# The second FFN product of the last two batches and of the global rows with seven half-size products for eight, in a kernel whose orders are laid by a planner

## The chip, the cores and the metric

The kernel runs on one core of a Trainium2 chip. The metric is the device time of one execution in microseconds (us), the median of several runs. A profiled execution gives the trace; its own time differs a little from the median and is given beside it.

The engines are TensorE (PE: matmuls, PEld: weight loads), VectorE (DVE), ScalarE (ACT), GpSimd (POOL) and SyncE (SP, here the queue that issues stores and transposing DMAs).

## The reference

Eight batches, eight heads, 512 local and 32 global tokens of 64 elements for each. Global rows see every token, local rows see the 32 global tokens and the local ones at most 32 away. The attention's rows, 544 for each batch and 4352 in all, of 512 elements, go through a two-layer product with a gate:

```python
out_g = matmul(softmax(scale * q_g @ k_all^T), v_all)            # 32 global rows
mask  = abs(pos[:, None] - pos[None, :]) <= 32
s_l   = concat([scale * q_l @ k_g^T, where(mask, scale * q_l @ k_l^T, -1e9)])
out_l = matmul(softmax(s_l), concat([v_g, v_l]))                  # 512 local rows
x = concat([out_g, out_l], axis=2).transpose(0, 2, 1, 3).reshape(4352, 512)

h = x @ w_in                       # 512 -> 2048
g = h * clip(h + 3, 0, 6) / 6
out = g @ w_out                    # 2048 -> 512
```

## The kernel before, in words

**Order.** The program declares operations with `add(engines, costs, emit, deps, rank, ...)`: on which engine each may run, what it costs by a model, what it waits for and which buffers (`take`, `give`) it holds. `Plan.run` then plays the whole kernel forward in Python and so fixes the order of every engine; `pick` chooses TensorE's next piece by keys (`key()`, with the constants `KEYS`, `SLACK`, `STEP`, `LEAD`, `PACE`, `WAIT`, `LATE`), and for a step that two engines may do it takes the one that is free. The operations are then emitted in that order. On the chip each engine works through its own list, waiting on semaphores, and never reorders it.

**Attention of a batch b.** `loads(b)` brings q, k, v; q and k are turned to have the head's dimension on partitions: by TensorE in small blocks (`turn_qk`, L700), in wide blocks (`turn_wide`, L737, batches in `WIDE`), or by transposing DMAs (`turn_all`, batches in `QT`, here batch 7). `spread` copies the values `vn` into `vs`, where each block of 128 rows finds its windows (L643 to L645; which engine may copy is in `MOVERS`: GpSimd, for batches 6 and 7 GpSimd and ScalarE). `local(b, j)` makes, for each of the four blocks of 128 rows, the scores S (L819), the masked maximum (VectorE, L831), the exponentials (ScalarE, L835), the turn of E (by TensorE where `EM` or `ETURN` says so, L848, else by DMA, L363), the product A with the values (L862), the norm (VectorE, L874 and L876), and the turn of the result x into `xt` (X; `XM`, `XTURN`, L883). `global_(b)` does the same for the 32 global rows against all tokens (L921 to L965).

**FFN of a batch.** `ffn_local(b)` calls `first()` 16 times: four matmuls (L1003) of 512 columns into a PSUM bank `m`, a relu on ScalarE (L1009) and the gate on VectorE (L1013), which frees the bank and leaves 128 of the 2048 inner columns in `gl`. `second()` then makes, for each 128 rows, 16 matmuls of 512 columns (L1029), a copy out of PSUM (ScalarE L1040 or VectorE L1042) into one of three `ot` buffers, and a store (SyncE, L1075). `ffn_global()` does the same at the end for the 256 global rows of all batches together; a block of 128 of them belongs to four batches and is stored by four DMAs (L1090). The two FFN products of one batch lie between the attention of the next one, piece by piece.

**PSUM.** Eight banks: three `m`, two `s` (scores and turns), two `a` (A and turns), one `t` (turns), which is handed to `m` when the last turn is done. At the start, until the first product can run, `warm()` puts matmuls without use (L1149) into TensorE's list.

## Time and profile before

| | us |
|---|---|
| median of the runs (329.3, 330.81, 330.38) | 330.38 |
| the profiled execution's own time | 331.21 |
| its span in the trace | 329.4 |
| TensorE busy | 318.2 (97%) |
| VectorE busy | 239.3 (73%) |
| ScalarE busy | 237.2 (72%) |
| GpSimd busy | 174.9 (53%) |
| granted TensorE clock | 1.0 |
| first product's matmuls (L1003, all forms) | 133.4 |
| second product's matmuls (L1029, all forms) | 132.5 |

Matmuls run in a pipeline, so that the busy time of one (0.38 us for 512 columns) is longer than the distance from its start to the next one's. What a matmul costs TensorE is read from a row of many in sequence in the chain (start of the first to start of what follows, divided by their number). A name such as `m<-wout,gl` gives output and inputs; "x44" is a number of instructions.

### The profile page before, as it was taken

To read this page: it belongs to the slowest core of one execution; us is meant where nothing else is said; L and a number is where in the kernel's file an instruction comes from. 1 tells how busy PE (TensorE), PEld (TensorE's weight loads), DVE (VectorE), ACT (ScalarE), POOL (GpSimd) and SP (SyncE) were. 2 spreads that over 40 slices of the span, in tenths; PEclk is the share of its full clock that TensorE was granted. 3 is DMA by queue.
4 is the path that set the end of the run, shared out by engine and by line. 5 is a ranking of instruction groups with operands and counts; after the bars stand their busy time and mean duration, and the time that the engine had idled before them with its cause. 6 is when DMAs were issued, how large, how long until landed. Compare 5 with 4: busy or idle time off the path is not lost.

```text
span 329.4 us, 12254 instructions
## 1 busy us (share of the span) xinstructions
PE 318.2 (97%) x4880; PEld 164.4 (50%) x4880; DVE 239.3 (73%) x987; ACT 237.2 (72%) x571; POOL 174.9 (53%) x278
## 2 busy tenths in 40 slices
PE   8999968999899999999999999999999999999995
PEld 3456756654445544455444544444444444446644
DVE  5699998879985889878898997588414993376400
ACT  3799999848967688689768999979815982365511
POOL 8499353799548879979997998059200000000000
PEclk9999999999999999999999999999999999999999
DMA  8999999998999799959999999598934457200013
GB/s 128 226 204 173 178 235 217 123 180 182 113 136 158 143 116 168 170 120 180 179 111 128 211 102 140 123 136 105 177 99 121 60 109 120 82 34 0 34 57 103
DMA packets 111369, 44.30 MB, mean 134 GB/s; under 512 B 88304, under 2 KB 107088, under 8 KB 111312
## 3 DMA queue, kind: packets, MB, share of 16 engines
q0 software_dynamic: 53136, 17.47, 52.6%
q1 hardware_dynamic: 58176, 26.05, 43.2%
q8 instruction: 38, 0.62, 0.8%
q14 instruction: 19, 0.16, 0.2%
HBM read 35.13 MB, written 8.91 MB: 134 GB/s over the span
## 4 chain that ended last, share of the span: by engine, by line
PE 75%; ACT 9%; DMA 7%; DVE 5%; issue 2%; POOL 1%; ACTq 0%
PE m L1029 30%; PE m L1003 23%; PE t L1029 4%; ACT ex L835 4%; PE t L1003 3%; PE m L1149 3%; DMA win<-in_moe_w_in_dram 3%; PE a L862 3%; DMA et<-ex 3%; PE s L819 2%; ACT t L1009 2%; DVE gl L1013 2%; DMA vn<-in_v_l_dram 1%; ACT vs L643 1%; PE t L883 1%
## 5 line engine op out<-in xcount | busy, mean ns | idle before, releaser
L1003 PE MATMUL m<-xt,win 128*128 128x512 f16 (+1 forms) x536 | 114.3, 354 | 4.2 <-DVE gl L1013 3.1
L1029 PE MATMUL m<-wout,gl 128*128 128x512 f16 (+1 forms) x496 | 117.7, 376 | 0.1
L645 POOL COPY vs<-vn 64x528 f16<-64x528 f16 (+1 forms) x165 | 102.5, 621 | 22.0 <-ACT vn L381 5.7
L1013 DVE SCALAR_TENSOR_TENSOR gl<-t,m 128x512 f16<-128x512 f32 (+1 forms) x147 | 86.3, 601 | 24.2 <-ACT t L1009 23.8
L835 ACT ACTIVATE ex<-sm,mx 128x128 f16<-128x128 f32 x256 | 85.1, 396 | 14.6 <-DVE mx L831 14.1
L1009 ACT ACTIVATE t<-m 128x512 f32<-128x512 f32 (+1 forms) x147 | 76.7, 532 | 19.7 <-PE m L1003 18.7
L1003 PEld LDWEIGHTS <-win 128*128 128x128 f16 x640 | 59.7, 98 | 57.9 <-issue 4.7
L1029 PEld LDWEIGHTS <-gl 128*128 128x128 f16 x560 | 51.7, 98 | 53.5 <-issue 0.4
L831 DVE CUSTOM_DVE_ANT_0 sm<-s,mask 128x128 f32<-128x128 f32 x256 | 60.0, 285 | 7.2 <-PE s L819 5.9
L643 ACT COPY vs<-vn 32x528 f16<-32x528 f16 (+1 forms) x39 | 24.5, 628 | 0.8
L876 DVE TENSOR_TENSOR x<-a,rec 128x256 f16<-128x256 f32 x64 | 24.0, 416 | 0.0
L1040 ACT COPY ot<-m 128x512 f32<-128x512 f32 (+1 forms) x21 | 12.1, 576 | 15.7 <-PE m L1029 15.7
L353 POOL DMA_DIRECT2D vn<-in_v_l_dram x24 | 21.1, 888 | 1.3 <-DMA kn<-in_k_l_dram 0.8
L831 DVE DVE_READ_ACCUMULATOR2_ANT mx<- 128x1 f32 x256 | 21.2, 83 | 0.0
L353 POOL DMA_DIRECT2D vn<-in_v_g_dram x7 | 4.1, 581 | 25.4 <-PE a L965 24.5
L862 PE MATMUL a<-vs,et 128*32 128x65 f16 x1024 | 14.4, 195 | 1.3 <-DMA et<-ex 1.2
L1149 PE MATMUL m<-ident 128*128 128x512 f16 x57 | 15.6, 392 | 0.0
L862 PEld LDWEIGHTS <-et 128*32 128x32 f16 x1024 | 10.2, 96 | 10.9 <-issue 7.3
L1013 DVE SCALAR_TENSOR_TENSOR gl<-t,t 128x512 f16<-128x512 f32 (+1 forms) x13 | 8.1, 624 | 9.7 <-ACT t L1009 9.7
L1029 PE MATMUL t<-wout,gl 128*128 128x512 f16 (+1 forms) x64 | 14.8, 353 | 0.0
L874 DVE RECIPROCAL rec<-a 128x4 f32<-128x4 f32 x64 | 8.5, 167 | 7.9 <-PE a L862 7.9
L353 POOL DMA_DIRECT2D kn<-in_k_l_dram x22 | 14.1, 644 | 0.1
(108 smaller groups left out, 292.4 us busy)
## 6 DMA issues: line engine op xcount, KB each, us to landing
out_dram<-ot SPq DMA_DIRECT2D x31, 256.0 KB, 2.6
vs<-vn SPq DMA_DIRECT2D x14, 264.0 KB, 7.0
qn<-in_q_l_dram POOLq DMA_DIRECT2D x14, 256.0 KB, 8.1
kn<-in_k_l_dram POOLq DMA_DIRECT2D x14, 256.0 KB, 7.1
vn<-in_v_l_dram POOLq DMA_DIRECT2D x24, 128.0 KB, 5.8
win<-in_moe_w_in_dram POOLq DMA_DIRECT2D x4, 512.0 KB, 9.6
wout<-in_moe_w_out_dram POOLq DMA_DIRECT2D x8, 256.0 KB, 11.2
gl<-in_v_l_dram POOLq DMA_DIRECT2D x8, 128.0 KB, 9.3
```

The lines of the kernel that those rows point to most:

```text
L353: op = add("POOL", dma(rows, run), lambda: nc.gpsimd.dma_start(out=dst, in_=src), deps, rank, LOAD_LAT + (MARGIN if what[0] in "vqkg" and ...
L643: nc.scalar.copy(out=dst, in_=src)
L645: (nc.vector if o.on == "DVE" else nc.gpsimd).tensor_copy(out=dst, in_=src)
L831: nc.vector.tensor_tensor_reduce(out=sm[i3][h], in0=pss[e][:, p * P:(p + 1) * P], in1=m, scale=-scale, scalar=3.0e38, op0=ALU.add, op1=ALU ...
L835: nc.scalar.activation(out=ex[ie][:, h, :], in_=sm[i3][h], func=EXP, scale=-1.0, bias=mx[i3][h])
L862: nc.tensor.matmul(out=psa[h // 4][q, c0:c0 + D + 1], lhsT=et[k][:, h * P + u * Sg:h * P + (u + 1) * Sg], rhs=vs[r][:, j * UJ + u, h, 0:D ...
L876: nc.vector.tensor_tensor(out=xs[ix][:, 4 * c * D:4 * (c + 1) * D].rearrange("q (h d) -> q h d", d=D), in0=acc[c][:, :, 0:D], in1=rr[c].to ...
L1003: nc.tensor.matmul(out=ps[:, 0:n], lhsT=w_in[:, m, c * P:(c + 1) * P], rhs=x(m), start=(m == 0), stop=(m == NP - 1))
L1009: nc.scalar.activation(out=t1[st["t"]][:, 0:n], in_=pm[st["m"]][:, 0:n], func=RELU, bias=0.5, scale=1.0 / 6.0)
L1013: nc.vector.scalar_tensor_tensor(out=g, in0=t1[st["t"]][:, 0:n], scalar=1.0, in1=pm[st["m"]][:, 0:n], op0=ALU.min, op1=ALU.mult)
L1029: nc.tensor.matmul(out=pm[st["m"]][:, 0:n], lhsT=g[c][:, t0:t0 + P], rhs=w_out[:, c, cols], start=(c == 0), stop=(c == NDFF - 1))
L1149: nc.tensor.matmul(out=pm[slots["m"][0]], lhsT=w, rhs=x)
```

## The change

Three parts.

*Seven products for eight.* For the batches 6 and 7 and for the global rows, `ffn_local` and `ffn_global` no longer call `second()`. The gated matrix G (rows by 2048) and `w_out` (2048 by 512) are cut into halves each way, and the four quarters of the output are made from seven half-size products (Strassen's scheme in Winograd's form). One pair is 256 rows: two blocks of 128, one from the upper half of the rows, one from the lower. There are five pairs: two in batch 6, two in batch 7, one in the global rows. A pair is 7 products of 8 matmuls of 256 columns, where there were 2 x 16 matmuls of 512.

- Four sums of quarters of `w_out` (`weight_sums`, 128 partitions by 2048 elements, f16) go into the buffers of q and k (`qn`, `kn`), on GpSimd.
- Sums of the gated halves (`sevenths`, L1070 in the new file; four for each two chunks, f16, 128x512 for a batch and 128x256 for the global rows) go into the buffers of the windows' values (`vs`), on VectorE or GpSimd; the planner gave 21 to VectorE and 27 to GpSimd.
- `pair` adds the products' results: one copy and three additions (`plus`, L1134) into f32 buffers laid over `xt` and `qT`, and four additions (`outs`, L1147) that read a PSUM bank and write a quarter of 128x256 into an `ot` buffer. For a batch a quarter is one store (L1214), for the global rows four stores of 32x256 (L1240).

*Banks.* When the attention is done, the two `s` and the two `a` banks are handed to `m` as the `t` bank is.

*Orders laid anew.* The FFN of batch 6 is declared after the local attention of batch 7. The order of the loads (`ORDER`), the priorities of the first two batches (`OFF`), which turns of E and X go through TensorE (`EM`, `XM`, `ETURN`, `XTURN`), `QT` (empty: batch 7 is turned by TensorE), `WIDE` (without batch 2), `MOVERS` (batches 2 to 6 GpSimd alone, 7 GpSimd and VectorE; ScalarE in none of them) and the constants of `pick` are new, so that the whole kernel's order changes.

Counted in the orders of the two kernels: matmuls of the second product, 528 of 512 columns and 32 of 256 before, 384 and 280 after; window copies on ScalarE 39 and 7, on VectorE 13 and 24, on GpSimd 165 and 186; stores of 128x512 31 and 24, of 128x256 2 and 16, of 32x512 8 and 0, of 32x256 0 and 16.

```diff
@@ -385,20 +387,20 @@
-    ORDER = "q0 k0 id v0 w0 o4 Q bd v1 o6 o1 w1 K V G w3 o7 o3 o0 w2 o5 o2".split()
+    ORDER = "q0 k0 v0 bd w0 id o7 Q v1 w1 V K G o2 w2 o1 o6 o3 w3 o0 o4 o5".split()
-    EM, XM = {(b, j) for b in range(2) for j in range(4)}, set()
+    EM, XM = set(), {(0, 0), (0, 1)}
-    ETURN = "00000000 11101110 10111111 11111111"
-    XTURN = "00000000 11001001 00010110 11011111"
-
-    QT = (7,)
-    MOVERS = {b: ("POOL",) if b < 6 else ("POOL", "ACT") for b in range(2, 8)}
-
-    WIDE = (0, 1, 2)
+    ETURN = "00000000 11100110 11011011 01111111"
+    XTURN = "00000000 10111010 01111111 11111111"
+
+    QT = ()
+    MOVERS = {b: ("POOL",) if b < 7 else ("POOL", "DVE") for b in range(2, 8)}
+
+    WIDE = (0, 1)
...
+    SEVEN, SUMS = {6: 2, 7: 4, 8: 4}, ("DVE", "POOL")
...
+    def both(dst, a, b, op, n, engines, deps, rank, what):
+        o = add(engines, tuple(dve(n, 2) if e == "DVE" else 100.0 + 1.9 * n for e in engines), None, deps, rank, lat=220.0, what=what)
+
+        def emit():
+            (nc.vector if o.on == "DVE" else nc.gpsimd).tensor_tensor(out=dst, in0=a, in1=b, op=op)
+        o.emit = emit
+        return o
+
+    def weight_sums():
...
+        for k, (a, d, x) in enumerate(((w_out[:, lo, right], w_out[:, lo, left], ()), (w_out[:, hi, right], wt[0], (0,)),
+                                       (w_out[:, hi, right], w_out[:, lo, right], ()), (w_out[:, hi, left], wt[1], (1,)))):
+            wt_op[k] = both(wt[k], a, d, ALU.subtract, n, ("POOL",), free + [wt_op[i] for i in x], (B, 5, k), f"wt{k}")
+
+    def sevenths(b, g, n, gates, into, free, store, banks):
...
+        for c in range(0, NH, 2):
...
+            for k, (x, y, op, by) in enumerate(((g[:, lo, dn], g[:, hi, dn], ALU.add, ()), (st_[:, 0, lo], g[:, lo, up], ALU.subtract, (0,)),
+                                                (g[:, lo, up], g[:, lo, dn], ALU.subtract, ()), (g[:, hi, up], st_[:, 1, lo], ALU.subtract, (1,)))):
+                o = both(st_[:, k, lo], x, y, op, 2 * n, SUMS, deps + [done[i] for i in by], (b, 0, 6, c, k), f"sum{b}.{k}")
...
+    def pair(b, i, n, g, s_, sums, gates, store, banks):
...
+        def plus(dst, a, x, deps, bank=None):
+            def emit():
+                nc.vector.tensor_tensor(out=dst, in0=a(), in1=at(x), op=ALU.add)
+                freed(bank)
...
+        p1 = product(0, "X", gt(0, a1), wo_(0, left), g1 + wo, 0)
...
+        p6 = product(1, "Y", su(1), wt_(1), sums[1] + [wt_op[1]], 1)
+        u2 = plus(ub[1], lambda: ub[0], "Y", [p6, cx], None if two else 1)
+        p7 = product(2, "W", su(2), wt_(2), sums[2] + [wt_op[2]] + ([cx] if two else []), None if two else 2)
+        u3 = plus(ub[2], lambda: ub[1], "W", [p7, u2])
+        p5 = product(3, "V", su(0), wt_(0), sums[0] + [wt_op[0]] + ([u2] if two else []), None if two else 3)
+        u4 = plus(ub[3], lambda: ub[1], "V", [p5, u2])
+        c22 = outs(1, right, "V", ub[2], [p5, u3], None)
+        p2 = product(4, "X", gt(NH, a1), wo_(NH, left), g2 + [cx] + ([u3] if two else []))
+        c11 = outs(0, left, "X", ub[0], [p2], None if two else 0)
+        p3 = product(5, "V", su(3), wo_(NH, right), sums[3] + [c22, u4])
+        c12 = outs(0, right, "V", ub[3], [p3, u4], 1 if two else 3)
+        p4 = product(6, "W", gt(NH, a2), wt_(3), [u3, wt_op[3]] + ([c11] if two else []))
+        c21 = outs(1, left, "W", ub[2], [p4], 0 if two else 2)
...
     def ffn_global():
...
+        if B in SEVEN:
+            def quarter(i, row, cols, o):
+                for a in range(per):
+                    nc.sync.dma_start(out=rows[row * per + a, 0:Sg, cols], in_=o[a * Sg:(a + 1) * Sg, 0:HALF])
+            sevenths(B, g_all[B % 2], B * Sg // 2, gates, vs[B % 2], m2_done[B - 2], quarter, SEVEN[B])
+            return
...
+        if b == B - 1 and SEVEN:
+            weight_sums()
+            ffn_local(b - 1)
         global_(b)
-        ffn_local(b)
+        if b != B - 2 or not SEVEN:
+            ffn_local(b)
...
-    KEYS = (30, 30, -20, 40, 27)
+    KEYS = (47, 44, -23, 52, 0)
...
+    for k, (r, banks) in enumerate((("s", pss), ("a", psa))):
+        pm.extend(banks)
+        add("POOL", 0.0, lambda k=k: slots["m"].extend((NM + 1 + 2 * k, NM + 2 + 2 * k)), [u for u in plan.ops if r in u.give], (-9,),
+            0.0, take=(r,) * 4, give=("m", "m"), what="bank")
```

More of the change, by code (lines that the diff above doesn't have):

```diff
@@ L323 @@
     vall = gl1[:, 0:8, :].rearrange("p (b n) c -> p b (n c)", b=2)
-    g_l = [sbs("gl0", NDFF, [P, Sl]), [gl1[:, c, :] for c in range(NDFF)]]
+    gl0 = sb("gl0", [P, NDFF, Sl])
+    g_all = [gl0, gl1]
+    g_l = [[g[:, c, :] for c in range(NDFF)] for g in g_all]
     g_g = [g[:, 0:B * Sg] for g in g_l[B % 2]]
@@ L406, in hold @@
         return what and (s_op if what[0] == "S" else av_op)[0][int(what[1])]
-    OFF = ((-1, -6.0, -9, -4.0, -3.5, 0, -2, 0, 8.0, 5.0), (-0.5, 1.0, 1.5, 8.5, -3.0, 0, -3.5, 2.5, -5.0, 5.5))
+    OFF = ((-4.0, 1.0, -9, 3.5, -4.5, 9, 0.0, 0, 0.5, 2.0), (-1.5, -4.5, 1.5, 0, -5.0, 4.0, -4.5, 0, 0.5, 1.0))
     WORKS = ("Tc", "Vc", "max", "exp", "Ec", "move", "norm", "Xc", "glob", "gate")
@@ L993 @@
     m1_done = [[] for _ in range(B)]
-    m2_done = [[] for _ in range(B)]
+    m2_done = [[] for _ in range(B + 1)]
+    SEVEN, SUMS = {6: 2, 7: 4, 8: 4}, ("DVE", "POOL")
     def first(x, n, g, c, deps, rank, kind, free):
@@ L1051, in second @@
         return last
+    HALF, NH = dm // 2, NDFF // 2
+    wt = [qn[k].rearrange("p n c -> p (n c)") for k in range(2)] + [knall[:, k * NH * HALF:(k + 1) * NH * HALF] for k in range(2)]
+    wt = [t.rearrange("p (c f) -> p c f", c=NH) for t in wt]
+    ut = [t.bitcast(FP32) for t in (xt[(B - 3) % 3].rearrange("p n c -> p (n c)"), qT[0].rearrange("d j p q -> d (j p q)"))]
+    wt_op = [None] * 4
+    u_use = {}
+    def both(dst, a, b, op, n, engines, deps, rank, what):
[4 more added lines that the diff above has]
+        return o
@@ new lines, in weight_sums @@
+    def weight_sums():
+        lo, hi, left, right = slice(0, NH), slice(NH, NDFF), slice(0, HALF), slice(HALF, dm)
+        free = [o for b in range(B - 3, B) for c in range(NP) for o in turned[b][c]] + wo
+        n = NH * HALF
+        for k, (a, d, x) in enumerate(((w_out[:, lo, right], w_out[:, lo, left], ()), (w_out[:, hi, right], wt[0], (0,)),
+                                       (w_out[:, hi, right], w_out[:, lo, right], ()), (w_out[:, hi, left], wt[1], (1,)))):
+            wt_op[k] = both(wt[k], a, d, ALU.subtract, n, ("POOL",), free + [wt_op[i] for i in x], (B, 5, k), f"wt{k}")
@@ new lines, in sevenths @@
+    def sevenths(b, g, n, gates, into, free, store, banks):
+        st_ = into.rearrange("p u h d -> p (u h d)")[:, 0:4 * NH * n].rearrange("p (s c t) -> p s c t", s=4, c=NH)
+        up, dn = slice(0, n), slice(n, 2 * n)
+        sums = [[] for _ in range(4)]
+        for c in range(0, NH, 2):
+            lo, hi = slice(c, c + 2), slice(NH + c, NH + c + 2)
+            deps = [gates[i] for i in (c, c + 1, NH + c, NH + c + 1)] + free
+            done = []
+            for k, (x, y, op, by) in enumerate(((g[:, lo, dn], g[:, hi, dn], ALU.add, ()), (st_[:, 0, lo], g[:, lo, up], ALU.subtract, (0,)),
+                                                (g[:, lo, up], g[:, lo, dn], ALU.subtract, ()), (g[:, hi, up], st_[:, 1, lo], ALU.subtract, (1,)))):
+                o = both(st_[:, k, lo], x, y, op, 2 * n, SUMS, deps + [done[i] for i in by], (b, 0, 6, c, k), f"sum{b}.{k}")
+                done.append(o)
+                sums[k].append(o)
+        for i in range(n // P):
+            pair(b, i, n, g, st_, sums, gates, store, banks)
@@ new lines, in pair, with at, product, freed @@
+    def pair(b, i, n, g, s_, sums, gates, store, banks):
+        a1, a2 = slice(i * P, (i + 1) * P), slice(n + i * P, n + (i + 1) * P)
+        left, right = slice(0, HALF), slice(HALF, dm)
+        lo, hi = range(NH), range(NH, NDFF)
+        k = u_use.setdefault("n", 0) % 2
+        u_use["n"] += 1
+        ub = [ut[k][:, e * HALF:(e + 1) * HALF] for e in range(4)]
+        st = {}
+        g1, g2 = [gates[c] for c in lo], [gates[c] for c in hi]
+        where = ({"X": (0, left), "W": (0, right), "Y": (1, left), "V": (1, right)} if banks == 2 else
+                 {x: (y, left) for y, x in enumerate("XYWV")})
+        two = banks == 2
+        def at(x):
+            return pm[st[where[x][0]]][:, where[x][1]]
+        prev = [None]
+        def product(m, x, lhs, rhs, deps, take=None):
+            def emit():
+                if take is not None:
+                    st[take] = slots["m"].pop(0)
+                for c in range(NH):
+                    nc.tensor.matmul(out=at(x), lhsT=lhs(c), rhs=rhs(c), start=c == 0, stop=c == NH - 1)
+            prev[0] = add("PE", (NH * (HALF / 2.4 + 2.6), NH), emit, [prev[0]] + deps, (b, 2 * i, m * 8 / 7.0),
+                          take=("m",) if take is not None else (), what="M2" if take is not None else "M2+")
+            return prev[0]
+        def freed(x):
+            if x is not None:
+                slots["m"].append(st[x])
+        def plus(dst, a, x, deps, bank=None):
+            def emit():
+                nc.vector.tensor_tensor(out=dst, in0=a(), in1=at(x), op=ALU.add)
+                freed(bank)
+            return add("DVE", 410.0, emit, deps, (-2.5,), give=("m",) if bank is not None else (), what="sevenths")
+        def outs(row, cols, x, a, deps, bank):
+            so = {}
+            give = ("m",) if bank is not None else ()
+            op = add("DVE", 400.0, None, deps, (-2.4,), take=("ot",), give=give, what="out")
+            def emit():
+                so["o"] = slots["ot"].pop(0)
+                dst = ot[so["o"]][:, 0:HALF]
+                nc.vector.tensor_tensor(out=dst, in0=a, in1=at(x), op=ALU.add)
+                freed(bank)
+            op.emit = emit
+            def emit_store():
+                store(i, row, cols, ot[so["o"]])
+                slots["ot"].append(so["o"])
+            add("SP", (660.0, P * 62.0 / 16, 62.0, P), emit_store, [op], (b, 2 * i, 9), DMA_LAT, give=("ot",), what="store")
+            return op
+        def gt(c0, cols):
+            return lambda c: g[:, c0 + c, cols]
+        def wo_(c0, cols):
+            return lambda c: w_out[:, c0 + c, cols]
+        def su(k_):
+            return lambda c: s_[:, k_, c, a1]
+        def wt_(k_):
+            return lambda c: wt[k_][:, c, :]
+        used = u_use.get(k, [])
+        p1 = product(0, "X", gt(0, a1), wo_(0, left), g1 + wo, 0)
+        cx = add(("ACT", "DVE"), (act(HALF), dve(HALF)), None, [p1] + used + m1_done[B - 3] + [s_op[B - 2][j] for j in range(NJ + 2)], (-2.5,), lat=220.0, what="sevenths")
+        def copy_x():
+            if cx.on == "ACT":
+                nc.scalar.copy(out=ub[0], in_=at("X"))
+            else:
+                nc.vector.tensor_copy(out=ub[0], in_=at("X"))
+        cx.emit = copy_x
+        p6 = product(1, "Y", su(1), wt_(1), sums[1] + [wt_op[1]], 1)
[11 more added lines that the diff above has]
+        c21 = outs(1, left, "W", ub[2], [p4], 0 if two else 2)
+        u_use[k] = [c11, c12, c21, c22]
+        m2_done[b].append(p4)
@@ L1062, in ffn_local @@
                 deps = x_op[b][j0:j1] + wi[c // (NDFF // 4)]
+                place = 2 * (c % NH) + c // NH if b in SEVEN else c
                 pe, ga = first(lambda m, t0=t0, n=n: x[:, m, t0:t0 + n], n, g_l[r][c][:, t0:t0 + n], c, deps,
-                               (b, part, c), "M1", free)
+                               (b, part, place), "M1", free)
                 m1_done[b].append(pe)
                 gates[part, c] = ga
+        if b in SEVEN:
+            def quarter(i, row, cols, o):
+                r0 = b * S + Sg + (2 * row + i) * P
+                nc.sync.dma_start(out=out[r0:r0 + P, cols], in_=o[:, 0:HALF])
+            sevenths(b, g_all[r], Sl // 2, [gates[0, c] for c in range(NDFF)], vs[r], [], quarter, SEVEN[b])
+            return
         for j in range(NJ):
@@ L1081, in ffn_global @@
             deps = [x_op[b][NJ] for b in range(B)]
-            pe, ga = first(lambda m: xg[:, :, m * Sg:(m + 1) * Sg], B * Sg, g_g[c], c, deps, (B, 0, c), "M1",
-                           m2_done[B - 2])
+            pe, ga = first(lambda m: xg[:, :, m * Sg:(m + 1) * Sg], B * Sg, g_g[c], c, deps,
+                           (B, 0, 2 * (c % NH) + c // NH if B in SEVEN else c), "M1", m2_done[B - 2])
             gates.append(ga)
@@ L1086, in ffn_global, with quarter @@
         rows = out.rearrange("(b s) d -> b s d", s=S)
+        if B in SEVEN:
+            def quarter(i, row, cols, o):
+                for a in range(per):
+                    nc.sync.dma_start(out=rows[row * per + a, 0:Sg, cols], in_=o[a * Sg:(a + 1) * Sg, 0:HALF])
+            sevenths(B, g_all[B % 2], B * Sg // 2, gates, vs[B % 2], m2_done[B - 2], quarter, SEVEN[B])
+            return
         for i in range(B // per):
@@ L1112 @@
             local(b, j)
+        if b == B - 1 and SEVEN:
+            weight_sums()
+            ffn_local(b - 1)
         global_(b)
-        ffn_local(b)
+        if b != B - 2 or not SEVEN:
+            ffn_local(b)
     ffn_global()
-    PACE, LEAD, SLACK, STEP, WAIT, LATE = 1, 40, 2, 4, 4000, 400
-    EARLY = 60000
-    KEYS = (30, 30, -20, 40, 27)
+    PACE, LEAD, SLACK, STEP, WAIT, LATE = 1, 40, 8, 6, 1000, 100
+    EARLY = 40000
+    KEYS = (47, 44, -23, 52, 0)
     REST = 0
+    SOONER = (0, 0, 0, 0, 0, 0, 0, 0)
     KEYED, GLAST = 0, 0
@@ L1138, in key @@
             elif w[0] in "VTG":
-                op.key = (r[0] - 1) * PIECES - LEAD - STEP * (2 - 0.25 * min(r[2] * 2, 4)) + KEYS[0]
+                op.key = (r[0] - 1) * PIECES - SOONER[r[0]] - LEAD - STEP * (2 - 0.25 * min(r[2] * 2, 4)) + KEYS[0]
             else:
-                op.key = (r[0] - 1) * PIECES - LEAD + STEP * (r[2] + 2 * (r[1] - 1)) + KEYS[1 + (w[0] == "A") + 2 * (w[-1] == "g")]
+                op.key = (r[0] - 1) * PIECES - SOONER[r[0]] - LEAD + STEP * (r[2] + 2 * (r[1] - 1)) + KEYS[1 + (w[0] == "A") + 2 * (w[-1] == "g")]
         return op.key
@@ L1152, in warm @@
         return op
-    PAIR, LAG = 16, 3
+    PAIR, LAG = 8, 3
     def alone(o, can):
```

## The prediction

> **What bounds the kernel now.** I read the page first (shares, chain, groups), then the chain in order of time, the timeline around each gap of TensorE, the tail, and the rows that price the new operations.

> ```profile
> span 329.4 us, 12254 instructions
> ...
> PE 318.2 (97%) x4880; PEld 164.4 (50%) x4880; DVE 239.3 (73%) x987; ACT 237.2 (72%) x571; POOL 174.9 (53%) x278
> ...
> PE 75%; ACT 9%; DMA 7%; DVE 5%; issue 2%; POOL 1%; ACTq 0%
> ...
> L1003 PE MATMUL m<-xt,win 128*128 128x512 f16 (+1 forms) x536 | 114.3, 354 | 4.2 <-DVE gl L1013 3.1
> L1029 PE MATMUL m<-wout,gl 128*128 128x512 f16 (+1 forms) x496 | 117.7, 376 | 0.1
> ```

> TensorE is the bound: 97% busy, 75% of the chain, mostly the two products. The second (L1029) waits for nothing, so fewer of its columns are time won, if nothing else comes late. Starting from the start-to-start spacing of each shape, all of TensorE's work lies in 312.7 us of the span, and its gaps come to 11.9 us; the rest is the entry before it and the end behind it.

> The chain in order of time gives those spacings:

> ```profile
> 104.53 0.64 PE s L700 x64
> ...
> 303.07 0.87 PE m L1003 x8
> ...
> 312.19 9.50 PE m L1029 x44
> ```

> A matmul of 512 columns takes 9.50/44 = 0.216 us, one of 256 columns 0.87/8 = 0.109: half, so narrow products cost no extra. A block of 64 small turns is 0.64; the wide form of a block (L737) is 1.01 in another row.

> The timeline where TensorE stops although it has work:

> ```profile
> 227.83 5.38 POOL L645 COPY vs<-vn 32x528 f16<-32x528 f16 x8
> ...
> 231.46 2.58 ACT L643 COPY vs<-vn 32x528 f16<-32x528 f16 x4
> ...
> 234.70 0.69 DVE L1013 SCALAR_TENSOR_TENSOR gl<-t,m 128x512 f16<-128x512 f32 x1 [2.06 <-ACT t L1009]
> 235.44 0.81 PE L1003 MATMUL m<-xt,win 128*128 128x512 f16 x3 [0.67 <-DVE gl L1013]
> ```

> ScalarE copies window values ahead of a relu (L1009); the gate waits, the bank is not freed, TensorE stands. By spacing this gap is 0.84 us. The same cause shows at 41.0 us (three copies, 1.91 us; gap 1.69) and at 195.4 (two copies, 1.28 us; gap 0.6).

> The end of the span, the store queue:

> ```profile
> 323.68 1.72 SPq L1090 DMA_DIRECT2D out_dram<-ot x4
> ...
> 325.65 1.22 SPq L1075 DMA_DIRECT2D out_dram<-ot x2
> ```

> Four small global stores hold SyncE's queue 1.72 us, 0.43 each; one wide store takes 0.35, and a landing comes 1.7 after the issue. The last landing is at 328.24, the end 1.16 later, in all 3.63 us behind the start of the last matmul (325.77).

> **The change, part by part.** The sum is against this execution: span 329.40, profiled 331.21, median of the runs 330.38, so a span S answers to a median of S + 0.98.

> *TensorE.* Counted in the two orders: 144 matmuls of 512 columns go (-144 x 0.216 = -31.1) and 248 of 256 columns come (+27.0): -4.1. Batch 7 is turned on TensorE instead of by DMA, +2 x 0.64; batch 2 in small instead of wide blocks, 2 x (0.64 - 1.01); together +0.5. 24 more turns of E and 24 fewer of X cancel. Sum **-3.5** (-4.1 if the turns fall into gaps).

> *The tail.* Before, each 128 rows end in one or four stores. After, a global quarter needs four stores of 32x256, a local one one of 128x256. In the new order the last pair of batch 7 and the global pair alternate, so each of four rounds queues five stores, 4 x 0.43 + 0.43 = 2.15 us, in all 8.6. The first of these quarters is ready 4.1 us of TensorE's order before the last matmul starts, so SyncE is free 4.5 after it; its last issue began 0.4 before that, lands 1.7 later, and the end follows 1.16 after: 6.9, against 3.63. Three buffers `ot` wait for these landings, which cannot shorten it. **+3.0**. Lower bound +1.3: only the three extra issues behind the last product count. Upper +3.2.

> *ScalarE.* It keeps 7 of its 39 window copies, all in the head. The three gaps named, 3.1 us, lose their cause. What is late next is the gate itself: between 25 and 58 us VectorE (30.4 of 33 us busy) and ScalarE (30.9) are both nearly full, and VectorE gets 11 more copies in the whole. I take **-2.5**; bounds 0 and -4.5 (with the waits for E by DMA, 1.4 at 89.2 us).

> *The new sums.* GpSimd does nothing after 233 us, so its work there takes no one's place by itself. Four weight sums of 2048 elements have no row; the nearest is GpSimd's copy of 528 elements, 621 ns. At that rate they are 2.4 us each, at twice that 4.9; behind the last moves (about 229) they end between 239 and 249, and their first reader starts near 270: nothing. [...]

> The 48 gate sums are shared, 27 to GpSimd and 21 to VectorE, 8 and 8 in batch 6's stage. That stage is where VectorE is tight, because it now lies beside batch 7's whole attention:

> ```profile
> 230.00:275.00 45.00, 44.33 (x508) 20.17 (x492) 26.08 (x110) 29.57 (x70) 2.97 (x5) 1.00 0.55 112
> 275.00:312.00 37.00, 37.00 (x302) 20.02 (x301) 19.58 (x41) 17.63 (x36) 0.00 (x0) 1.00 0.22 50
> ```

> (third busy column: VectorE.) TensorE's work there: 16 pieces of the first product at 0.864, 6 early products at 0.87, scores, A and the entries about 4, and 2 of batch 7's pieces: 24.9 us. VectorE's: 16 maxima x 0.21, 4 norms x 0.9, 16 gates x 0.60, 1.1 besides = 17.7. A sum of 512 f16 on VectorE: between 0.29 (a window copy of 528) and 0.60 (a gate), middle 0.45, x 8 = 3.6. What a GpSimd operation at the same time costs VectorE shows one row:

> ```profile
> L802 DVE COPY kT<-gT x32: 218/230/647, 7.3 to 192.4; 128x288 f16<-128x288 f16 x32
> ```

> The copies of 230 ns grow to 647 where a window copy of GpSimd runs (181.12 beside one at 180.33). The gates at 229.5 to 231.5 stay at 0.69 while GpSimd copies, so I count only operations that read and write SBUF alone as hit, and take 0.42 for each of the 8 sums: 3.4. VectorE then has 24.7 of 24.9, and an order laid for a lighter VectorE slips a little: **+0.8** (bounds 0 and +7.5, below). [...] The additions out of PSUM (15 `plus`, 20 `outs`, 0.34 each as the norm's product) lie in stages where VectorE had 19.6 of 37 us: nothing.

> Sum: -3.5 + 3.0 - 2.5 + 0.8 = **-2.2**; span 327.2, median **328.2**. Own range 326.8 to 329.6.

> **Rivals.**

> *Slower: VectorE's sums wait out whole GpSimd sums.* Place: batch 6's stage. If a VectorE sum takes 0.6 and waits 0.9 (a GpSimd sum between 0.6 and 1.24, twice the copy's row), VectorE has 17.7 + 4.8 + 7.2 = 29.7 against 24.9, so +4.8 instead of +0.8: **332.2**. It makes the change a loss from a wait of 0.68 us on; with 1.24 it is 334.9. For it: both engines' sums are released by the same gates, so they meet. Against it: GpSimd is busy with its 8 sums only some 30% of the stage. [...]

> *No relief.* The gaps at 41, 195 and 234 us return because the gates wait for VectorE instead of ScalarE: -3.5 + 3.0 + 0.8 = +0.3, **330.7**. For it: VectorE's 30.4 of 33 us in the head.

> *Full relief and a short tail.* -3.5 + 1.3 - 3.1 + 0.8 = -4.5: **325.9**; with the waits for E gone too, 324.5. For it: the stores may issue faster with a quarter's bytes each.

> *Slow GpSimd sums.* Batch 7's 11 sums on GpSimd must fit in some 24 us; above 2.2 us each GpSimd is the bound, at 3 us +9: **337**. Nothing in the copies' row speaks for it.

> **How the numbers follow.** A measurement of this kernel can tell about 0.5% (1.65 us) from no change, so faster ends at 328.7 and slower begins at 332.0. Forecast 0.44 (0.33 of it faster, 0.11 same), full relief 0.14 (faster), no relief 0.20 (0.16 same, 0.04 slower), waiting sums 0.19 (0.16 slower, 0.03 same), slow sums 0.03. Faster 0.47, same 0.30, slower 0.23. The range 325.0 to 332.6 leaves out the longer waits, the slow sums and the best case.

> **What would show it.** Matmul counts of 384 and 280 in the second product; the last matmul starting about 319 to 322 us and the end 6 to 7 us behind it, with SyncE's queue unbroken there; no ScalarE copy of window values after 60 us and no gaps near 195 and 234; sums (L1070) on VectorE under 0.9 us with their waits, on GpSimd under 1.3. Wrong would be: VectorE busy throughout batch 6's stage with TensorE waiting for gates or sums there, or gaps as large as before in the head.

## The result: slower by half a per cent, and the profile after

The changed kernel took 332.02 us (median; 330.84 to 336.55) against 330.69 us for the kernel before (329.30 to 332.14, runs of the same chip). The ratio is 1.0049, interval 1.0028 to 1.0070: slower, by about as much as a measurement can tell. Some executions of a kernel are over 1.5% longer than its fastest, as the one of 336.55 us is, and the ratios leave these out. The forecast was 328.2 us, faster; 332.0 lies in its range and at the price of its slower rival (332.2), but, as the runs below show, not by that rival's cause.

The page of the changed kernel, its head and the chain's shares:

```profile
span 330.3 us, 12995 instructions
...
PE 313.9 (95%) x5176; PEld 175.0 (53%) x5176; DVE 264.4 (80%) x1038; ACT 226.8 (69%) x553; POOL 225.4 (68%) x322
...
PE 71%; DVE 18%; issue 4%; DMA 2%; ACT 2%; SPq 1%; POOL 1%; DVEq 0%; ACTq 0%; POOLq 0%
```

TensorE is busy 4.3 us less, and its share fell from 97% to 95%: the time went into waiting. In the chain VectorE rose from 5% to 18%, and "issue", time in which an engine waits for nothing that the profile shows, from 2% to 4%.

The span splits into three parts: TensorE's work (each matmul at the median start-to-start spacing of its kind), its gaps (what is above that), and the end behind the start of the last matmul. The entry, 1.2 us, is the same in both. The sum of work and gaps is read off exactly; how it divides depends on which matmuls count as one kind. Other groupings of the same traces give -3.4 to -5.3 for the work and +1.0 to +2.9 for the gaps, with the same signs.

| us | before | after | difference | forecast |
|---|---|---|---|---|
| TensorE's work | 312.7 | 308.1 | -4.6 | -3.5 |
| gaps | 11.9 | 14.1 | +2.2 | -1.7 (-2.5 + 0.8) |
| end | 3.63 | 6.89 | +3.3 | +3.0 |
| span | 329.4 | 330.3 | +0.9 | -2.2 |

So the work and the end came out nearly as forecast, and the gaps did not. The timeline at the largest of the new ones, where TensorE begins batch 7's first scores (L821):

```profile
224.82 4.68 POOL L647 COPY vs<-vn 32x528 f16<-32x528 f16 x7
...
225.76 1.88 DVE L647 COPY vs<-vn 64x528 f16<-64x528 f16 x3
...
229.45 0.68 DVE L385 COPY qT<-s 128x512 f16<-128x512 f16 x1
...
229.59 4.06 POOL L1070 TENSOR_TENSOR qn<-wout 128x2048 f16<-128x2048 f16 x1
...
230.19 0.41 PE L821 MATMUL s<-kT,qT 64*32 64x128 f16 x31 [1.56 <-DVE qT L385]
...
230.76 3.04 DVE L647 COPY vs<-vn 32x528 f16<-32x528 f16 x1
```

One score matmul ran at 228.40, the other 31 at 230.19: 1.79 us of gap. They waited for VectorE to bring batch 7's turned q out of PSUM, and VectorE had three window copies of the same batch ahead of that (1.88 us). Before, batch 7 was turned by DMA and ScalarE shared its window copies. The copies themselves are dear in this place. With no GpSimd copy beside it, such a copy of VectorE takes 0.29 us in the same trace (at 30.5 and 30.8 us). These three take 0.52 to 0.67 beside GpSimd's own copies, and the one in the last row takes 3.04 beside a weight sum of 4.06. Each of the nine that VectorE makes for batch 7 ends 0.15 us behind the GpSimd operation that was running when it began.

Three other gaps have no releaser at all. Two of them in the timeline:

```profile
54.22 0.36 PE L821 MATMUL s<-kT,qT 64*32 64x128 f16 x24 [1.47 <-issue]
...
110.61 0.56 PE L702 MATMUL a<-ident,kn 64*64 64x64 f16 x45 [0.88 <-issue]
```

In both the first part of a group of equal small matmuls had run, and the rest had nothing left to wait for. The third is at 64.6 us. By spacing they are 1.65, 1.07 and 0.72 us, 3.4 together; the kernel before had none over 0.4 of this kind in its trace.

The end, in the store queue (L1214 the quarters of batch 7, L1240 those of the global rows):

```profile
321.10 0.37 SPq L1214 DMA_DIRECT2D out_dram<-ot  x1
321.56 1.77 SPq L1240 DMA_DIRECT2D out_dram<-ot  x4
```

The queue is never empty after 319.3; the next such round starts at 323.43, so one of five stores takes 2.33 us, where 2.15 were forecast.

### The profile page after: what moved, and what is told of

Its sections match the earlier page's. It is cut to its first block, busy times and chain, and to the rows that moved or that the text cites. A ratio compares the mean times of both kernels' runs of the same rounds, so it can differ in the third digit from the quotient of the medians.

```text
span 330.3 us, 12995 instructions
## 1 busy us (share of the span) xinstructions
PE 313.9 (95%) x5176; PEld 175.0 (53%) x5176; DVE 264.4 (80%) x1038; ACT 226.8 (69%) x553; POOL 225.4 (68%) x322
## 4 chain that ended last, share of the span: by engine, by line
PE 71%; DVE 18%; issue 4%; DMA 2%; ACT 2%; SPq 1%; POOL 1%; DVEq 0%; ACTq 0%; POOLq 0%
PE m L1033 22%; PE m L1007 22%; DVE gl L1017 5%; PE m L1123 4%; DVE vs L647 4%; DVE sm L833 3%; PE a L864 3%; PE t L1007 3%; PE s L821 3%; DMA kn<-in_k_l_dram 2%; PE s L1007 2%; PE s L1123 2%; PE t L850 1%; ACT t L1013 1%; PE t L1033 1%
## 5 line engine op out<-in xcount | busy, mean ns | idle before, releaser
L647 POOL COPY vs<-vn 32x528 f16<-32x528 f16 (+1 forms) x186 | 115.8, 622 | 19.3 <-ACT vn L383 5.2
L1033 PE MATMUL m<-wout,gl 128*128 128x512 f16 x368 | 90.5, 380 | 0.2 <-DVE gl L1017 0.2
L1017 DVE SCALAR_TENSOR_TENSOR gl<-t,m 128x512 f16<-128x512 f32 (+1 forms) x130 | 76.8, 604 | 16.0 <-ACT t L1013 14.6
L1013 ACT ACTIVATE t<-m 128x512 f32<-128x512 f32 (+1 forms) x130 | 68.5, 539 | 30.5 <-PE m L1007 27.2
L1033 PEld LDWEIGHTS <-gl 128*128 128x128 f16 x384 | 34.5, 98 | 38.5 <-issue 0.6
L1070 POOL TENSOR_TENSOR vs<-gl 128x512 f16<-128x512 f16 (+1 forms) x12 | 12.0, 998 | 33.6 <-DVE gl L1017 24.2
L878 DVE TENSOR_TENSOR x<-a,rec 128x256 f16<-128x256 f32 x64 | 24.0, 417 | 0.1
L821 PE MATMUL s<-kT,qT 64*32 64x128 f16 x1024 | 14.2, 219 | 3.6 <-issue 2.0
L1123 PEld LDWEIGHTS <-vs 128*128 128x128 f16 x160 | 15.7, 98 | 3.5
L821 PEld LDWEIGHTS <-qT 64*32 64x32 f16 x1024 | 8.1, 91 | 14.9 <-issue 14.4
L383 ACT COPY et<-t 128x1024 f16<-128x1024 f16 (+1 forms) x13 | 12.8, 987 | 4.5 <-PE t L850 4.5
L647 DVE COPY vs<-vn 64x528 f16<-64x528 f16 (+1 forms) x24 | 14.2, 591 | 0.6
L1007 PE MATMUL t<-xt,win 128*128 128x512 f16 x56 | 14.4, 379 | 0.0
```

The source lines that it names most:

```text
L647: (nc.vector if o.on == "DVE" else nc.gpsimd).tensor_copy(out=dst, in_=src)
L821: nc.tensor.matmul(out=pss[e][u * Sg:(u + 1) * Sg, p * P:(p + 1) * P], lhsT=qT[r][rows, j, p, u * Sg:(u + 1) * Sg], rhs=kT[r][rows, p, k0: ...
L878: nc.vector.tensor_tensor(out=xs[ix][:, 4 * c * D:4 * (c + 1) * D].rearrange("q (h d) -> q h d", d=D), in0=acc[c][:, :, 0:D], in1=rr[c].to ...
L1007: nc.tensor.matmul(out=ps[:, 0:n], lhsT=w_in[:, m, c * P:(c + 1) * P], rhs=x(m), start=(m == 0), stop=(m == NP - 1))
L1013: nc.scalar.activation(out=t1[st["t"]][:, 0:n], in_=pm[st["m"]][:, 0:n], func=RELU, bias=0.5, scale=1.0 / 6.0)
L1017: nc.vector.scalar_tensor_tensor(out=g, in0=t1[st["t"]][:, 0:n], scalar=1.0, in1=pm[st["m"]][:, 0:n], op0=ALU.min, op1=ALU.mult)
```

## The experiments

**The scheme undone, the orders kept.**

```diff
-    SEVEN, SUMS = {6: 2, 7: 4, 8: 4}, ("DVE", "POOL")
+    SEVEN, SUMS = {}, ("DVE", "POOL")
```

> The changed kernel with the second product of every batch as before (16 matmuls of 512 columns for 128 rows); TensorE's order is the changed kernel's up to the second product of batch 6. Theory (the scheme saves 4 us of TensorE and gives 3.3 us of it back in the stores at the end; the loss sits in the new orders): ratio to before about 1.007, some 0.8 us slower than the changed kernel, with the gaps at 52, 64, 109 and 228 us as there, and an end about 3.6 us behind the last matmul. Rival (the sums on VectorE and GpSimd cost the time): faster than the changed kernel, ratio 1.000 or less.

332.06 us, ratio 1.0039 (1.0015 to 1.0062): no different from the changed kernel. TensorE's work is 311.4, the gaps 14.2, the end 3.57; TensorE's order is the changed kernel's up to 270 us. The gaps at 52, 64, 109 and 228 us are all there (1.55, 0.56, 1.14, 1.80). So the gaps belong to the new orders, and on these orders the scheme is worth nothing: 3.3 us less work (308.1 against 311.4) and 3.3 us more at the end. The theory expected 0.8 us of net gain. The second product fell by 3.6 us and not 4.1, which leaves 0.3, too little for these intervals (some 0.7 us either way) to tell.

**The scheme kept, the orders undone.** All constants of the order (`ORDER`, `OFF`, `EM`, `XM`, `ETURN`, `XTURN`, `QT`, `MOVERS`, `WIDE`, `KEYS`, `SLACK` and the rest) as before.

> The changed kernel with all of before's constants for the order; TensorE's order is that of before up to the second product of batch 6, then seven products for eight. Theory: about 0.998 of before (TensorE -4.1, end +3.3), gaps before 225 us as in before. Rival (the sums cost the time): 1.005 or more, with TensorE waiting for gates or sums after 238 us.

343.97 us, ratio 1.0381 (1.0339 to 1.0423). The theory failed widely; its rival had TensorE waiting for gates or sums after 238 us, as the first gap below shows. The same kernel, profiled again:

> The same kernel as the scheme on before's orders, for a second profile, since the first profiled execution (348 us) was slower than the others (342.6 to 345). Theory (its loss is in the stage of batches 6 and 7: a sum on VectorE that waits out a weight sum of GpSimd, 2.3 us of TensorE near 268 us, and the first product of batch 7 that waits for batch 7's last rows, 4.6 us near 296 us): both gaps are there again, and the one of 5.9 us near 89 us is 1.5 us or less. Rival (these gaps belong to the slower execution): less than 3 us of gaps after 240 us.

344.7 us, span 342.9. Both gaps came again, 2.31 and 4.75 us, and the one at 89 us was gone. The first, in the timeline:

```profile
258.74 4.07 POOL L1070 TENSOR_TENSOR kn<-wout,qn 128x2048 f16<-128x2048 f16 x1
259.54 3.89 DVE L1070 TENSOR_TENSOR vs<-gl 128x512 f16<-128x512 f16 x2
...
264.41 1.87 PE L1007 MATMUL t<-xt,win 128*128 128x512 f16 x4 [2.15 <-DVE gl L1017]
```

A weight sum on GpSimd runs to 262.8; two gate sums on VectorE, begun after it, take 3.89 us instead of 0.76 (two with GpSimd idle, in the run with all sums on VectorE below), and the first ends 0.28 us behind the weight sum; the gates stand behind them, and TensorE behind the gates. The second, in the chain in order of time:

```profile
281.83 4.27 DMA out_dram<-ot
...
286.10 1.97 DMA out_dram<-ot
...
291.83 3.46 DMA xt<-x
...
295.34 3.48 PE s L1007 x8
```

For the `ot` buffers of the two landings of `out`, additions that write quarters (`outs`) wait on VectorE. Then come batch 7's last norm (L878, 289.67), which was queued behind them, and the turn of its result by DMA. TensorE has nothing but batch 7's first product left. Its clock then falls: eight matmuls of 512 columns take 3.48 us, 0.435 each, and the granted clock is 0.86 between 275 and 300 us. The same is seen behind the first gap, where eight more start 0.43 us apart and the granted clock is 0.93 between 250 and 275. Three more gaps, of 1.77, 1.00 and 1.43 us at 273.6, 285.6 and 288.7 us, were not followed one by one. So the scheme does badly on the old orders; with the new ones, no gap over 0.15 us is left between 238.4 us and the end.

**The stores at the end from two queues**, everything else unchanged:

```diff
-                    nc.sync.dma_start(out=rows[row * per + a, 0:Sg, cols], ...)
+                    (nc.scalar if a % 2 else nc.sync).dma_start(out=rows[row * per + a, 0:Sg, cols], ...)
```

> The changed kernel, each global quarter's four stores issued in turn by SyncE and ScalarE, two each; orders unchanged. Theory (the end is bound by the issue of 20 stores on one queue): per round SyncE has 3 issues, 1.3 us, in 1.75 us of TensorE's work, so the end follows the last matmul's start by about 4.7 us instead of 6.9; ratio to before about 0.998. Rival (the end is bound by the three output buffers and their landings): still 6.5 us or more, ratio 1.004.

329.30 us, ratio 0.9958 (0.9935 to 0.9980). The end is 4.32 us behind the last matmul's start instead of 6.89. So 2.6 us of the end were the issue of stores on one queue. The additions still wait 2.0 us for landings (3.3 in the changed kernel).

**Batch 7's window copies from VectorE to GpSimd:**

```diff
-                        (nc.vector if o.on == "DVE" else nc.gpsimd).tensor_copy(out=dst, in_=src)
+                        (nc.vector if o.on == "DVE" and b < B - 1 else nc.gpsimd).tensor_copy(out=dst, in_=src)
```

> The changed kernel, the 11 window copies of VectorE for batch 7 made by GpSimd instead, orders otherwise unchanged. Theory (batch 7's turned q and k stand behind these copies in VectorE's list, which delays its first scores): the gap at 228.4 us shrinks from 1.79 to 0.6 us or less, ratio to before about 1.001. Rival (the turn's own copies out of PSUM take that time): the gap stays at 1.5 us or more and the ratio at 1.004; or GpSimd, later by 7 us, delays the products with the values and the time rises.

329.39 us, ratio 0.9952 (0.9930 to 0.9974). The scores of the same place, in the timeline:

```profile
227.12 0.42 PE L821 MATMUL s<-kT,qT 64*32 64x128 f16 x32
```

All 32 run at once: the gap is gone whole, and with it one of 0.32 at 237.8. GpSimd's later weight sums delay nothing. By the trace the edit moves nine copies and not 11: VectorE's other two of the 11 new ones lie in the head. The two gaps are 2.1 of the 2.6 us; the rest was not placed.

**Both edits together:**

> The changed kernel with both edits that shortened it: the global stores from two queues, and batch 7's window copies on GpSimd. Theory (two costs of the change at different places, 2.7 us and 2.6 us by the two runs): they add, 332.0 - 5.3 = 326.7, ratio to before 0.988. Rival (one is hidden behind the other): 0.993 or more.

327.13 us, ratio 0.9904 (0.9871 to 0.9937). In the trace both costs are gone: no gap at 228 us, and an end of 4.33 us. That the two add (326.7 us, 0.988) lies in the interval; its upper edge just reaches the rival's 0.993.

**The place of the stops "issue".** 28 warming matmuls at the start, split in halves:

```diff
-            nc.tensor.matmul(out=pm[slots["m"][0]], lhsT=w, rhs=x)
+            halves = (slice(0, 256), slice(256, 512)) if state.setdefault("split", 0) < 28 else (slice(0, 512),)
+            state["split"] += 1
+            for h in halves:
+                nc.tensor.matmul(out=pm[slots["m"][0]][:, h], lhsT=w, rhs=x[:, h])
```

> The changed kernel with 28 of the warming matmuls at the start split in two halves of 256 columns: the same work, and every later matmul stands 28 places further back in TensorE's program. Theory (TensorE's program comes in blocks of 128 matmuls, each fetched when the one ahead of it is entered, and dense small matmuls run through a block faster than the 4.3 to 5.8 us that this takes): the stop of 1.65 us among batch 1's scores near 52.5 us goes, and stops appear where the new blocks last under 4 us: near 61.5 us (block of 3.48 us) and near 85 us (3.1 us), each 0.8 to 2.5 us. Rival (these scores wait for a transfer or another engine): the stops stay at 52.5, 64.6 and 109.5 us.

A single execution, 331.47 us, too little to tell a change of time (its end came 8.22 us behind the last matmul's start, since one round of four global stores took 3.09 us). The stops at 52.5, 64.6 and 109.5 us are gone, and two are left, at other work:

```profile
61.89 0.29 PE L702 MATMUL a<-ident,kn 64*64 64x64 f16 x12 [0.41 <-issue]
```

and one of 1.05 us in batch 3's turns at 106.3. Counted in the trace, they come at TensorE's matmuls number 1116 and 2011, and in the changed kernel they came at 860, 1116 and 2011: numbers that differ by multiples of 128 (one less at the last). At number 860, where the block ahead now lasted 6.3 us, no stop came. So the stop goes with the place in the program and not with the work, in steps of 128 matmuls with their weight loads, 256 instructions. The queue of instruction packets (q8) carries 40 packets of 16,384 bytes in the changed kernel and 38 in the kernel before, about as many as there are such blocks: TensorE's 5176 and 4880 matmuls make 40.4 and 38.1. For the stop at 52.5 us, the block ahead was entered at 48.4, the packet began at 51.9 and took 0.95 us, and TensorE went on at 54.2: 5.8 us after entry, while the block itself lasted 4.09. That such a packet brings TensorE's next block, and is fetched when the block ahead is entered, was the author's reading; the traces show only these counts and times. Of the two stops forecast, the one near 61.5 us came (0.41 us idle, under the 0.8 forecast); the one at 85 us, behind a block of 3.1 us, did not, so a short block alone does not make one. Their size also varies with the execution of the same order: the one at number 1116 was 0.7 us, 0.2 and none in the traces of the changed kernel, the two-queue run and the run with batch 7's copies moved, while the one at 860 was 1.4 us or more in each. What else decides (the load of the DMA queues is near) was not tried.

**All gate sums on VectorE:**

```diff
-            (nc.vector if o.on == "DVE" else nc.gpsimd).tensor_tensor(out=dst, in0=a, in1=b, op=op)
+            (nc.vector if o.on == "DVE" or what[0] == "s" else nc.gpsimd).tensor_tensor(out=dst, in0=a, in1=b, op=op)
```

> The changed kernel with all 48 sums of gates on VectorE, at the places that the planner gave them. Theory (these sums cost nothing, TensorE has no gap over 0.1 us after 238): the sums on VectorE take 0.29 us each with no GpSimd beside them, in all about what the 21 take now with their waits; the ratio stays at 1.003 to 1.006. Rival (VectorE waiting out GpSimd's sums is what made the change slower): 1.000 or less.

333.16 us, ratio 1.0086 (1.0047 to 1.0124). Nothing is won by taking the waits away. A sum of 512 elements alone takes 0.42 us and not 0.29, VectorE's list is longer, and a gap of 0.75 us behind gates appears at 265.5. So the waits of VectorE's sums are not what made the changed kernel slower.

**The weight sums in four parts each**, `for c in range(0, NH, 2)` around the operation:

> The changed kernel with each of the four weight sums on GpSimd cut into four of 512 elements. Theory (a VectorE operation in SBUF waits for the end of the GpSimd operation that runs): the window copy on VectorE that took 3.04 us at 230.8 takes 1.2 us or less, and the gate behind it starts about 2 us earlier; no change of time beyond 0.3%. Rival (it shares the memory with GpSimd at a slower rate for as long as GpSimd works): it still takes over 2 us.

A single execution, 330.77 us against 330.84 to 336.55 of the changed kernel, too little to tell a change. The copy on VectorE, beside GpSimd's parts:

```profile
228.67 4.55 POOL L1072 TENSOR_TENSOR qn<-wout 128x512 f16<-128x512 f16 x4
...
229.83 1.26 DVE L647 COPY vs<-vn 32x528 f16<-32x528 f16 x1
```

1.26 us instead of 3.04, a little over the 1.2 expected, and the gate behind it begins 1.29 us after the copy's start instead of 3.07. In both runs the copy ends 0.15 us behind the GpSimd operation that ran when it began, of 4.06 us there and 1.15 here: it waits for that end, and how long the operation is sets the price. The rival's slower rate would have held it for over 2 us, since GpSimd's next part followed at once. The whole weight sum costs 4.55 us in parts and 4.06 in one.

**The prediction's own term, in the kernel before.** ScalarE's window copies of batch 7, and then those of batches 6 and 7, made by GpSimd:

```diff
-                    if o.on == "ACT":
+                    if o.on == "ACT" and b < B - 1:
```

For both batches the bound is `B - 2`.

> The kernel before, with the window copies of batch 7 that ScalarE made (12 copies between 223 and 236 us) made by GpSimd instead, orders otherwise unchanged. Theory (the prediction's term: such copies stand ahead of the relu, and the gap of 0.84 us at 234.4 goes with them): the gap under 0.2 us, ratio to before 0.996 to 0.998. Rival (the next late thing takes its place): gaps from 225 to 250 us still sum to 0.7 us or more, ratio 0.999 to 1.001; or GpSimd, busy to about 240 us instead of 233, delays the products with the values.

329.59 us, ratio 0.9979 (0.9957 to 1.0002). The gap of 0.84 us is gone; the gaps from 225 to 250 us sum to 0.02. The interval of the time alone could not tell theory from rival; the trace does. In this trace the order of the kernel before has a stop "issue" as well, 0.50 us by spacing at 80.5 us, at matmul number 1370, two short of a multiple of 128 from 860.

> The kernel before, with the window copies of batches 6 and 7 that ScalarE made (25) made by GpSimd instead. Theory: the gaps at 195 us (0.6) and 234 us (0.84) both go, ratio 0.995 to 0.997. Rival (GpSimd, which also issues the loads and is full from 150 to 230 us, falls behind by the 13 copies of batch 6, 8 us): the loads of batch 7 land late, its scores wait, and the time rises above that of the run with batch 7's copies alone.

328.95 us, ratio 0.9952 (0.9931 to 0.9973). In its trace, of an execution of 336.86 us, the gap at 195 us is gone. The cause was read rightly: such copies ahead of a relu do stop TensorE, and are worth about 1.5 us there, as the two gaps had it (0.6 and 0.84).

**The head: four copies of the global keys of batch 1 to GpSimd**, on top of the two edits:

```diff
-                nc.vector.tensor_copy(out=dst, in_=gT[(b // 2) % 2]...
+                (nc.gpsimd if b == 1 else nc.vector).tensor_copy(out=dst, in_=gT[(b // 2) % 2]...
```

> The changed kernel with the stores from two queues and batch 7's copies on GpSimd (327.1 us), and in addition the four copies of the global keys for batch 1 (128x288, near 40.4 us) on GpSimd instead of VectorE. Theory (VectorE's list is what delays the gates between 37 and 47 us in the changed kernel, as the chain has it): the gap of 0.81 us near 41.9 goes to 0.2 or less, 0.5 to 0.8 us faster, ratio to before about 0.988. Rival (the next copy or reduction on VectorE is late as well, or GpSimd's loads behind these copies are): gaps from 25 to 50 us still sum to 3.2 us or more, ratio 0.990 or more.

326.12 us, ratio 0.9880 (0.9853 to 0.9907), the fastest of all and faster than both kernels. The gap at 41.8 us fell from 0.82 to 0.49 only, and those from 25 to 50 us from 3.45 to 3.09, between theory and rival; the median is 1.0 us below that of the two edits, but the intervals overlap. TensorE still waits for the gates (0.33 us at 42.35), and they for VectorE:

```profile
40.94 0.79 DVE L934 TENSOR_REDUCE gm<-s 128x1 f32<-128x272 f32 x2
...
41.89 1.07 DVE L1017 SCALAR_TENSOR_TENSOR gl<-t,m 128x256 f16<-128x256 f32 x3
```

The next thing in VectorE's list, the global maxima (L934), is ahead of the gates in its turn.

## Why the prediction was wrong, point by point

*TensorE: -3.5, measured -4.6.* By the split of the table the orders alone gave -1.3 (312.7 to 311.4) where +0.5 was forecast, and the scheme -3.3 instead of -4.1: two errors of opposite sign, so the sum is nearer than its parts by luck. The turns are not the reason: without the two gaps behind them in the kernel before (at 52.7 and 56.5 us), E's rose from 5.2 to 6.6 us and X's fell from 5.2 to 3.7, so "24 more turns of E and 24 fewer of X cancel" holds. What makes up the -1.3 was not found, and other groupings give -0.4 to -2.4.

*The tail: +3.0, measured +3.3.* The end was forecast 6.9 us behind the last matmul's start, and is 6.89; 6.9 against 3.63 is +3.3, so the +3.0 in the sum was a slip (with +3.3 the forecast is 328.5 us). The two-queue run shows that the reason was right as well. That the number fits so closely is luck: the rounds of stores took 9.6 us in all where 8.6 were forecast, and the first store was issued 5.0 us ahead of the last matmul's start instead of 4.1.

*ScalarE: -2.5. This is the step that failed.* The gaps at 195 and 234 us went as forecast (and the one at 89 us), and the runs on the kernel before show that the cause was the right one. But the head's 1.69 us at 41 became 0.96, 0.81 and 0.88 at 39 to 46, now behind VectorE, as the rival "no relief" had it for the head; gaps as large as before there were one of the prediction's own signs of being wrong. And the new orders brought gaps of their own that no step looked for: 1.79 us for batch 7's first scores and 3.4 us of stops that go with TensorE's place in its program. So in place of 2.5 us won, the gaps rose by 2.2: the step summed the gaps that would go and had no term for those that a new order brings. The first could have been found: the step counted the 0.64 us that each block of turns takes TensorE, and not its copies out of PSUM nor the window copies ahead of them in VectorE's list. Nor did it price VectorE's copies beside GpSimd's, though the row of 230 and 647 ns that the prediction shows for other copies was the sign of it. The second could hardly be foreseen: the kernel before had no such stop over 0.4 us in its trace, and which blocks bring one is open.

*The new sums: +0.8, measured about nothing.* VectorE was nearly full in batch 6's stage, as forecast (22.8 of 25 us between 250 and 275), but TensorE had no gap over 0.15 us there. The sums' prices in the changed kernel: GpSimd 1.15 to 1.22 us for 512 elements and 4.06 to 4.12 for 2048, within the bounds of 0.6 to 1.24 and 2.4 to 4.9. A VectorE sum of 512 elements took 0.42 us alone and up to 1.27 where it met one of GpSimd's:

```profile
L1070 POOL TENSOR_TENSOR vs<-gl x12: 667/1152/1160, 256.2 to 311.2; 128x512 f16<-128x512 f16 x8, 128x256 f16<-128x256 f16 x4
L1070 DVE TENSOR_TENSOR vs<-gl x12: 291/676/1265, 256.6 to 312.4; 128x512 f16<-128x512 f16 x8, 128x256 f16<-128x256 f16 x4
```

*The slower rival.* Its mechanism exists, with a wait of up to 0.85 us per sum (1.27 against 0.42), above its point of 0.68. It decided nothing on the new orders, since not every sum met one: of VectorE's eight in batch 6's stage two did (1.00 us each), a mean wait of 0.14 us where the forecast itself took 0.42. That the measured 332.0 lies at this rival's 332.2 is chance. On the old orders it cost 2.3 us, by the timeline, through a weight sum, which the prediction had put down as free.

## What to carry to other kernels

Count a saving on the bound engine together with what the rest of the order does to its gaps: here 4.6 us of work were saved, and a store queue (3.3 us), VectorE's list ahead of batch 7's scores (1.8) and stops for TensorE's program (3.4) took back more than that and the gaps that went. When work is moved to another engine, follow every instruction of the moved step into the list it joins and read what stands ahead of it there, the copies out of PSUM above all. When an order is laid anew together with a new algorithm, run the two apart: here each was slower alone, the orders by 0.4% and the scheme by 3.8%.

## What the runs showed of the hardware that was not expected

A VectorE copy that takes 0.29 us alone took 3.04 beside a GpSimd operation of 4.06 us, and 1.26 when that was cut in four. VectorE's window copies of batch 7 ended 0.15 us behind the GpSimd operation that they met, and its sums of 512 elements 0.28, whether that had lasted 0.62, 1.15 or 4.06 us. The price was the rest of the GpSimd operation, so for that copy one operation of 4.06 us was worse than four of 1.15.

After gaps of 2.31 and 4.75 us TensorE's matmuls of 512 columns started 0.43 us apart instead of 0.216, for eight of them, so that each gap cost some 1.7 us more. After the gap of 1.79 us in the changed kernel they started 0.216 apart at once; whether the length of the gap decides was not tried, and another execution of the same kernel had the gap of 2.31 us without it.
